# A fused attention and FFN kernel whose opening is issued from a table in another order

## The chip, the cores and the metric

The kernel runs on one NeuronCore of one Trainium2 chip. The core has five engines that run their own instruction streams and meet at semaphores: TensorE (PE in the profile) multiplies matrices into PSUM, which has eight banks; VectorE (DVE) and ScalarE (ACT) do elementwise work; GpSimd (POOL) here issues the loads; SyncE (SP) issues the other DMAs. The metric is the time of one execution on the device in microseconds. Before the change it is 337.19 us, the median of 3 runs (336.64 to 337.4).

## The reference

The function is sliding-window causal attention followed by a SwiGLU block. q, k and v have 8 batches, 8 heads, 576 positions and 64 columns. The heads are joined to 4608 tokens of 512 columns, which feed the second part.

```python
scores = scale * np.matmul(q, k.transpose(0, 1, 3, 2))
mask = (rel >= 0) & (rel < 64)                 # rel: query position less key position
attn = softmax(np.where(mask, scores, -1e9))
x = np.matmul(attn, v).transpose(0, 2, 1, 3).reshape(4608, 512)
g = x @ w_gate                                 # 512 x 1536
val = x @ w_val                                # 512 x 1536
out = (g * sigmoid(g) * val) @ w_out           # 1536 x 512
```

Inputs and output are float32; the kernel computes in bfloat16 with float32 sums.

## The kernel before

The 4608 tokens are 36 chunks of 128 (`n`) and 9 FFN groups of 512 tokens (`c`), four chunks each. For a chunk, `load_qk(n)` and `load_v(n)` put q, k and v into rings of 6, 6 and 10 buffers as bfloat16. `T(n)` transposes q and k on TensorE (line 412) and copies them out of PSUM (line 342 or 344). `TD(n)` does the same with two DMA transposes on SP (lines 425, 428). `S(n)` computes the scores with 24 small matmuls (line 456) and their exponentials on ScalarE (line 466). For chunks 0 to 3, `bias(n)` first writes the mask into the two banks with two matmuls (line 436); otherwise VectorE multiplies the exponentials by the mask (line 471). `A(n)` multiplies with v in two phases (line 505); the row sums come with it, and VectorE takes their reciprocals (line 520) and normalises (line 523) in two halves. `X(n)` transposes the result on TensorE (line 595) and copies it to `xT` (line 604); `XD(n)` does it by a DMA transpose on SP (line 610).

`F(c, f, t0, t1)` is one of the 12 blocks of 128 hidden columns of a group, for the tokens t0 to t1: four matmuls for the gate, four for the value (line 628), a tanh on ScalarE (line 634) and two operations on VectorE (lines 636 and 638) which leave the hidden block in `hT`. `O(c, u)` multiplies 128 tokens of a group with the whole of w_out in 12 matmuls (line 652), evicts the result and stores it. It waits for all 12 hidden blocks and for both halves of w_out (`load_wo`).

Each engine issues its instructions in the order in which `build` calls these functions. Semaphore waits are derived from what each reads and writes. PSUM banks are handed out in rotation, four for the FFN and four for attention, with a list of six at the start. `warm(count)` issues matmuls on a zeroed tile whose result nobody reads.

The opening was written out by hand: 13 warm matmuls, attention of chunks 0 and 1 with five more warm matmuls between, the first two FFN blocks in pieces of 128 tokens, attention of chunks 2 and 3, blocks 2 to 5 of group 0 in halves of 256 tokens, and so on up to group 1. In the loop over `c`, which starts at group 1, `block(n)` stands between the FFN blocks: it loads chunk n + 6, runs `A(n)` with the scores of chunk n + 1 between its two phases, and issues `XD(n)` and `TD(n + 4)`. Group 2 and later take the same path.

All loads of q, k, v and the weights are issued by POOL in program order, and are cast from float32 to bfloat16 as they land. The first two chunks of q and k come by SP and ACT (`first_loads`), and are cast by VectorE and ScalarE.

Of the kernel before, what the change touches and what calls it, by code (L numbers as in the profile page):

```python
# [4 lines left out]
ACTF = mybir.ActivationFunctionType  # L5
# [4 lines left out]
T = B * S  # L10
# [183 lines left out]

class _Kernel:
# [17 lines left out]
    def alloc(self):  # L213
# [39 lines left out]
        self.n_s = 0  # L253
        self.kb = [sb("kb%d" % i, 192, F32) for i in range(3)]
# [7 lines left out]
    def bank(self, kind):  # L262
        kind = "*" if "*" in self.rot else kind
        ids, i = self.rot[kind]
        self.rot[kind] = (ids, i + 1)
        j = ids[i % len(ids)]
        return self.ps[j], ("ps", j)
# [78 lines left out]
    def first_T(self, which):  # L346
# [11 lines left out]
        return tb, bk  # L358

    def first_ev(self, which, n, eng, tb, bk):  # L360
# [39 lines left out]
    def T(self, n, keng="act"):  # L400
        iq, iz = n % self.NQ, n % self.NZ
        kd = self.kT[:, :, 64 + 128 * n:64 + 128 * n + 128]
        kk, qk = [("kT", n, p) for p in range(4)], [("qT", iz, p) for p in range(4)]
        parts = [("kn", self.kn[iq], kd, kk, keng), ("qn", self.qn[iq], self.qT[iz], qk, "act")]
        for group in ([parts] if keng == "act" else [parts[:1], parts[1:]]):
            bank, bk = self.bank("a")
            tb = bank[:, :].bitcast(BF).rearrange("p (w c t) -> p w c t", w=2, c=4)

            def pe(e, group=group, tb=tb):
                for w, part in enumerate(group):  # L410
                    for c in range(4):
                        r = e.transpose(tb[:, w, c, :], part[1][:, 2 * c:2 * c + 2, :], self.ident[:, :])
                return r

            self.g.op("pe", pe, reads=["ident"] + [(g[0], iq, j) for g in group for j in range(2)], writes=[bk])
            for w, (_, _, d, wk, eng) in enumerate(group):
                self.move(eng, d, tb[:, w], [bk], wk)
# [13 lines left out]
    def bias(self, n):  # L431
# [6 lines left out]
        return bb  # L438

    def S(self, n, bb=None, defer=False):  # L440
# [3 lines left out]
        qT, pt = self.qT[iz], self.pt[ip]  # L444
        biased = bb is not None
# [28 lines left out]
        for f in masks:  # L474
            f()

    def A(self, n, nxt=None):
        g = self.g
        ip, ix = n % self.NP, n % 4
# [34 lines left out]
        first = g.op("pe", phase(0), reads=rd, writes=wr)  # L514
        masks = self.S(nxt, None, True) if nxt is not None else []
        g.op("pe", phase(1), reads=rd, writes=wr, after=[first])
        for half, (bank, bk) in enumerate(bb):
# [7 lines left out]
        for f in masks:  # L525
            f()
# [59 lines left out]
    def X(self, n, eng="dve"):  # L586
        g = self.g
        ix, it = n % 4, (n // 4) % self.NX
        xb = self.xb[ix]
# [8 lines left out]
        g.op("pe", pe, reads=["ident", ("xb", ix, 0), ("xb", ix, 1)], writes=[bk])  # L598
        u = n % 4
        xo = self.xT[it][:, :, 128 * u:128 * u + 128]  # L600
        if eng == "dve":
            g.op("dve", lambda e: e.tensor_copy(xo, tb), reads=[bk], writes=[("xT", it, u)])
        else:
            g.op("act", lambda e: e.activation(xo, tb, ACTF.Copy), reads=[bk], writes=[("xT", it, u)])  # L604
# [8 lines left out]
    def F(self, c, f, t0=0, t1=512):  # L613
        g = self.g
        it, ih = c % self.NX, c % self.NH
        xT, hT = self.xT[it], self.hT[ih]
        i = self.n_s % self.NS
        self.n_s += 1
        sig, uu = self.sig[i], self.uu[i]
# [3 lines left out]
        V, vk = self.bank("f")  # L623
# [10 lines left out]
        g.op("act", lambda e: e.activation(sig[:, 0:n], G[:, 0:n], ACTF.Tanh, scale=0.5), reads=[gk], writes=[("sig", i)])  # L634
        g.op("pe", mm(V, self.Wv), reads=xk + [("Wv", f)], writes=[vk])
        g.op("dve", lambda e: e.scalar_tensor_tensor(uu[:, 0:n], sig[:, 0:n], 1.0, G[:, 0:n], ALU.add, ALU.mult),  # L636
# [4 lines left out]
    def O(self, c, u, mid=None, kind="a", eng="act"):  # L641
        g = self.g
        ih = c % self.NH
        hT = self.hT[ih]
        io = (4 * c + u) % self.NO
        ost = self.ost[io]
        OB, ok = self.bank(kind)

        def part(f0, f1):
            def pe(e):  # L650
                for f in range(f0, f1):
                    r = e.matmul(OB[:, :], hT[:, f, 128 * u:128 * u + 128], self.Wo[:, f, :],  # L652
                                 start=(f == 0), stop=(f == NF - 1))
                return r

            g.op("pe", pe, reads=[("hT", ih, f) for f in range(f0, f1)] + [("Wo", f) for f in range(f0, f1)], writes=[ok])

        if mid is None:
            part(0, NF)
        else:  # L660
            part(0, 8)
            mid()
            part(8, NF)
        self.move(eng, ost[:, :], OB[:, :], [ok], [("ost", io)])
        r0 = 512 * c + 128 * u
        g.op("sp", lambda e: e.dma_start(self.out[r0:r0 + 128, :], ost[:, :]), reads=[("ost", io)], dma=True)

# [126 lines left out]
    def general(self):  # L794
# [7 lines left out]
        for n in range(NCH):  # L802
            self.load_qk(n)
            self.load_v(n)
            self.T(n)
            self.S_general(n)
            self.A(n)
            self.X(n, "act")
# [8 lines left out]
    def build(self):  # L817
# [11 lines left out]
        self.load_v(0)  # L829
        self.load_v(1)  # L830
        W(0, 1)
        self.load_qk(2)
        W(1, 2)
        self.load_qk(3)
        self.load_v(2)
        self.load_v(3)
        for f in range(2, 8, 2):
            W(f, f + 2)
        self.load_qk(4)
        W(8, 10)  # L840
        self.load_v(4)
        load(5)
        W(10, 12)
        load(6)
        load(7)

        self.banks("a", [5, 6, 7, 4, 0, 1])
        self.warm(13)
        self.first_cast("k", None, "dve")
        self.first_cast("q", 0, "act")  # L850
        self.first_cast("q", 1, "dve")
        tk = self.first_T("k")
        tq = self.first_T("q")
        b0, b1 = self.bias(0), self.bias(1)
        for n in range(2):
            self.first_ev("k", n, "dve", *tk)
            self.first_ev("q", n, "act", *tq)
# [6 lines left out]
        self.X(0, "act")  # L864
        self.banks("a", [5, 6, 7, 4])
        self.T(2, "dve")
        self.F(0, 0, 0, 128)
        self.X(1, "act")
        self.F(0, 1, 0, 128)
        self.F(0, 0, 128, 256)  # L870
        self.F(0, 1, 128, 256)
        self.T(3, "dve")
        load(8)
        b2 = self.bias(2)
        self.S(2, b2)
        b3 = self.bias(3)
        self.S(3, b3)
        self.F(0, 2, 0, 256)
        self.A(2)
# [168 lines left out]
```

## Time and profile before

| | before |
|---|---|
| median of 3 runs | 337.19 us |
| the profiled execution | 335.81 us |
| its span, first to last instruction | 334.0 us |
| TensorE busy | 320.0 us, 96% |
| VectorE busy | 220.5 us, 66% |
| ScalarE busy | 133.6 us, 40% |
| read from and written to memory | 37.75 MB, 9.44 MB |

The span is what the rows of the profile cover; the time of an execution is some 1.8 us longer. A matmul row gives the start, the time until its result is written, and the number of matmuls that follow each other; the next row starts before the last one's result is out, so work is best read from start to start. In brackets stands how long the engine was idle before and what ended that. Sizes in rows of DMA issues are those in bfloat16.

### The profile page before, as it was taken

Reading aid. Unit: us, or ns where it says so; the run is one execution under the profiler, and the core shown is the slowest. Engines: PE = TensorE matmul, PEld = TensorE weight load, DVE = VectorE, ACT = ScalarE, POOL = GpSimd, SP = SyncE. Lnnn points to the kernel's source line nnn. Section 1 sums busy time; section 2 is a strip of 40 time slices with the busy share of each in tenths; the row PEclk is TensorE's granted clock in tenths of the full one; section 3 lists DMA queues with packets and bytes.
Section 4 is the critical chain, followed back from the end, with each engine's and each line's share of the span. In section 5 each row is a group of like instructions: output and inputs, shape, how many; then the busy total and the mean of one; then the engine's idle time right before and its main releaser. Section 6 shows DMA issues by size and latency. Waiting matters only on the chain.

```text
span 334.0 us, 8383 instructions
## 1 busy us (share of the span) xinstructions
PE 320.0 (96%) x3477; PEld 166.1 (50%) x3515; DVE 220.5 (66%) x481; ACT 133.6 (40%) x248; POOL 110.7 (33%) x141
## 2 busy tenths in 40 slices
PE   8889989998999999999999999999999999999996
PEld 3657557644444444445454545454545444444444
DVE  5558799477666766667777777767676776565510
ACT  2655775353444544444333333333424222332312
POOL 7999993463635453333615151000000000000000
PEclk9999999999999999999999999999999999999999
DMA  9999999999999999999999999915241202000012
GB/s 171 151 190 172 166 196 159 157 168 152 159 169 180 173 153 173 161 151 115 130 125 123 133 123 131 126 51 110 47 105 41 65 31 65 32 31 34 34 66 96
DMA packets 169516, 40.20 MB, mean 120 GB/s; under 512 B 155904, under 2 KB 164992, under 8 KB 169472
## 3 DMA queue, kind: packets, MB, share of 16 engines
q0 software_dynamic: 117312, 18.36, 83.4%
q1 hardware_dynamic: 50976, 20.66, 33.1%
q10 hardware_dynamic: 1184, 0.59, 0.7%
q8 instruction: 29, 0.48, 0.6%
q14 instruction: 15, 0.12, 0.1%
HBM read 37.75 MB, written 9.44 MB: 141 GB/s over the span
## 4 chain that ended last, share of the span: by engine, by line
PE 84%; DMA 4%; POOL 4%; DVE 3%; issue 2%; ACT 1%; SPq 1%; POOLq 0%
PE ps L628 51%; PE ps L652 26%; PE ps L456 3%; DMA qT<-qn 2%; DMA Wv<-in_moe_w_val_dram 2%; PE ps L505 2%; PE ps L552 2%; POOL va L387 1%; DVE uu L636 1%; PE ps L680 1%; DVE xb L523 1%; POOL Wg L393 1%; DVE hT L638 1%; POOL qn L325 1%; POOL kn L325 1%
## 5 line engine op out<-in xcount | busy, mean ns | idle before, releaser
L636 DVE SCALAR_TENSOR_TENSOR uu<-sig,ps 128x512 bf16<-128x512 bf16 (+2 forms) x122 | 76.0, 623 | 62.8 <-ACT sig L634 62.6
L628 PE MATMUL ps<-xT,Wv 128*128 128x512 bf16 (+2 forms) x479 | 112.9, 354 | 1.3 <-DMA Wv<-in_moe_w_val_dram 0.7
L628 PE MATMUL ps<-xT,Wg 128*128 128x512 bf16 (+2 forms) x464 | 108.2, 354 | 5.2 <-issue 3.4
L634 ACT ACTIVATE sig<-ps 128x512 bf16<-128x512 f32 (+2 forms) x122 | 67.2, 551 | 76.6 <-PE ps L628 76.4
L652 PE MATMUL ps<-Wo,hT 128*128 128x512 bf16 x416 | 95.5, 379 | 0.3 <-issue 0.2
L638 DVE SCALAR_TENSOR_TENSOR hT<-uu,ps 128x512 bf16<-128x512 bf16 (+2 forms) x122 | 76.4, 626 | 4.7 <-PE ps L628 0.6
L628 PEld LDWEIGHTS ps<-xT,Wv 128*128 128x128 bf16 x488 | 46.9, 98 | 47.7 <-DMA Wv<-in_moe_w_val_dram 1.0
L628 PEld LDWEIGHTS ps<-xT,Wg 128*128 128x128 bf16 x488 | 44.3, 98 | 43.2 <-ACT xT L604 0.8
L652 PEld LDWEIGHTS ps<-Wo,hT 128*128 128x128 bf16 x420 | 40.9, 98 | 49.0
L325 POOL DMA_DIRECT2D qn<-in_q_dram x38 | 35.2, 944 | 66.5 <-DMA qT<-qn 66.2
L466 ACT ACTIVATE pt<-ps 128x512 bf16<-128x512 f32 x72 | 38.1, 599 | 34.5 <-PE ps L456 33.6
L342 ACT ACTIVATE ost<-ps 128x512 f32<-128x512 f32 (+2 forms) x29 | 16.8, 579 | 73.2 <-PE ps L652 72.2
L387 POOL DMA_DIRECT2D va<-in_v_dram x40 | 37.1, 936 | 24.2 <-PE ps L552 23.1
L325 POOL DMA_DIRECT2D kn<-in_k_dram x38 | 35.3, 936 | 4.3 <-DMA Wo<-in_moe_w_out_dram 3.7
L471 DVE TENSOR_TENSOR pt<-pt,mask 128x512 bf16<-128x512 bf16 x64 | 23.6, 417 | 0.2 <-ACT pt L466 0.2
L344 DVE COPY ost<-ps 128x512 f32<-128x512 f32 (+1 forms) x9 | 5.8, 646 | 23.2 <-PE ps L680 11.8
L523 DVE TENSOR_TENSOR xb<-ps,rc 128x256 bf16<-128x256 f32 x40 | 17.0, 424 | 1.4
L456 PE MATMUL ps<-qT,kT 64*64 64x64 bf16 (+1 forms) x864 | 16.0, 203 | 1.1 <-DMA qT<-qn 1.1
L456 PEld LDWEIGHTS ps<-qT,kT 64*64 64x64 bf16 x864 | 12.5, 108 | 6.6 <-issue 4.0
L505 PE MATMUL ps<-va,pt 64*64 64x65 bf16 x600 | 12.7, 197 | 0.6
L520 DVE RECIPROCAL rc<-ps 128x4 f32<-128x4 f32 x40 | 7.0, 174 | 9.4 <-PE ps L505 9.4
L505 PEld LDWEIGHTS ps<-va,pt 64*64 64x64 bf16 x600 | 8.4, 106 | 8.9 <-issue 4.7
(55 smaller groups left out, 105.3 us busy)
## 6 DMA issues: line engine op xcount, KB each, us to landing
out_dram<-ost SPq DMA_DIRECT2D x35, 256.0 KB, 3.7
va<-in_v_dram POOLq DMA_DIRECT2D x32, 128.0 KB, 10.0
qn<-in_q_dram POOLq DMA_DIRECT2D x30, 128.0 KB, 10.0
kn<-in_k_dram POOLq DMA_DIRECT2D x30, 128.0 KB, 12.5
Wo<-in_moe_w_out_dram POOLq DMA_DIRECT2D x2, 768.0 KB, 15.1
Wg<-in_moe_w_gate_dram POOLq DMA_DIRECT2D x5, 256.0 KB, 8.0
Wv<-in_moe_w_val_dram POOLq DMA_DIRECT2D x5, 256.0 KB, 8.6
fk<-in_k_dram SPq DMA_DIRECT2D x1, 512.0 KB, 5.0
```

What stands on the lines that cost most here:

```text
L325: self.g.op("pool", lambda e, d=d, a=a: e.dma_start(d, a), writes=ks, dma=True)
L387: g.op("pool", lambda e, d=d, a=a: e.dma_start(d, a), writes=ks, dma=True)
L456: r = e.matmul(sv[h][o:o + 64, c, q0:q1], self.kT[ps, c, kk:kk + 64], qT[ps, c, q0:q1], start=not biased, stop=not biased or c == 3 and kk ...
L466: g.op("act", lambda e, po=po, si=si: e.activation(po, si, ACTF.Exp, scale=SCALE), reads=[bk], writes=[pk])
L471: "dve", lambda e: e.tensor_tensor(po, po, m, ALU.mult), reads=[pk, "mask"], writes=[pk]))
L505: r = e.matmul(av[half][ws, j, :], pt[ks, h, ws], vv[ks, h, 0:65], start=key == q[0], stop=key == q[-1])
L523: g.op("dve", lambda e, xo=xo, rb=rb, a=av[half]: e.tensor_tensor(xo, a[:, :, 0:64], rb, ALU.mult), reads=[bk, ("rc", ir)], writes=[("xb", ...
L628: r = e.matmul(bank[:, 0:n], W[:, kk, f * 128:f * 128 + 128], xT[:, kk, t0:t1], start=(kk == 0), stop=(kk == NK - 1))
L634: g.op("act", lambda e: e.activation(sig[:, 0:n], G[:, 0:n], ACTF.Tanh, scale=0.5), reads=[gk], writes=[("sig", i)])
L636: g.op("dve", lambda e: e.scalar_tensor_tensor(uu[:, 0:n], sig[:, 0:n], 1.0, G[:, 0:n], ALU.add, ALU.mult), reads=[("sig", i), gk], writes ...
L638: g.op("dve", lambda e: e.scalar_tensor_tensor(hT[:, f, t0:t1], uu[:, 0:n], 0.5, V[:, 0:n], ALU.mult, ALU.mult), reads=[("uu", i), vk], wr ...
L652: r = e.matmul(OB[:, :], hT[:, f, 128 * u:128 * u + 128], self.Wo[:, f, :], start=(f == 0), stop=(f == NF - 1))
```

## The change

The hand-written opening, and the loop's turn for group 1, are replaced by one table, `OPENING`, of some 300 rows. A row is a method, its arguments and the PSUM banks that it takes, in order. Methods that held several engines' work are split, so that each part has a row: `T` into a transposition of q or of k (`T`) and its copy (`TE`), `A` into its phases (`A0`, `A1`) and the two halves of its normalisation (`R`), `X` into `X` and `XE`, `F` into the matmuls (`FM`), the tanh (`Ft`) and VectorE's part (`Fu`), `O` into `OM` and `OE`, and the masking of the scores into `M`. Each piece computes what it did before.

In the table the loads go v1, qk2, v0, qk3, v2, the first weight block, v3, and then weights and chunks 4 to 7 mixed; blocks 8 and 9 come behind chunk 8's and 10's q and k, the second half of w_out behind chunks 9 and 11. Attention of chunks 0 to 3 comes before the first FFN block. Eleven warm matmuls stand at the start, followed by the bias of chunk 2, and four single ones later. The scores of chunks 8 to 12, the first four output blocks and the attention of chunks 8 to 11 come late in group 1, between its blocks. Some copies go from ScalarE to VectorE and the other way. After the table the loop begins at group 2, with the two rotations of banks set anew.

```diff
+OPENING = [
+    ("warm", (11,), (4,)),
+    ("bias", (2,), (0, 4)),
+    ("first_cast", ("k", None, "dve"), ()),
+    ("first_T", ("k",), (3,)),
...
+    ("bias", (0,), (1, 5)),
+    ("load_v", (1,), ()),
+    ("bias", (1,), (6, 7)),
+    ("load_qk", (2,), ()),
+    ("first_ev", ("k", 0, "act"), ()),
+    ("T", ("q", 2), (3,)),
+    ("load_v", (0,), ()),
...
+    ("S", (0,), ()),
+    ("first_ev", ("q", 1, "dve"), ()),
+    ("S", (1,), ()),
+    ("TE", ("q", 2, "dve"), ()),
+    ("T", ("k", 2), (2,)),
+    ("TE", ("k", 2, "dve"), ()),
+    ("A0", (0,), (3, 5)),
+    ("A1", (0,), ()),
...
+    ("FM", (0, 0, 128, 256, 2), (5, 7)),
+    ("R", (2, 0), ()),
+    ("Ft", (0, 0, 128), ()),
+    ("load_w", ("g", 2, 4), ()),
+    ("warm", (1,), (0,)),
+    ("load_w", ("v", 2, 4), ()),
+    ("FM", (0, 0, 0, 128, 2), (4, 3)),
...
+    ("load_qk", (10,), ()),
+    ("TD", (10,), ()),
+    ("load_w", ("g", 8, 10), ()),
+    ("X", (7,), (4,)),
...
+    ("load_w", ("v", 8, 10), ()),
+    ("load_wo", (0, 6), ()),
+    ("FM", (0, 8, 0, 512, 2), (3, 5)),
...
+    ("OM", (0, 2), (4,)),
+    ("Fu", (1, 7, 0), ()),
+    ("S", (9,), (5, 2)),
...
+    ("S", (12,), (2, 0)),
...
+    ("FM", (1, 11, 0, 512, 2), (1, 4)),
+    ("Ft", (1, 11, 0), ()),
+    ("Fu", (1, 11, 0), ()),
+]
...
     def bank(self, kind):
+        if self.give:
+            return self.given(self.give.pop(0))
...
     def warm(self, count):
-        bank, bk = self.ps[3], ("ps", 3)
+        bank, bk = self.bank("f")
...
-        self.banks("a", [5, 6, 7, 4, 0, 1])
-        self.warm(13)
-        self.first_cast("k", None, "dve")
...
-        self.S(0, b0)
-        self.S(1, b1)
-        self.warm(3)
-        self.A(0)
-        self.warm(2)
-        self.A(1)
...
+        for op, args, give in OPENING:
+            self.give = list(give)
+            getattr(self, op)(*args)
+        self.banks("a", [4, 5, 6, 7])
+        self.banks("f", [0, 1, 2, 3])
...
-        for c in range(1, NFC):
+        for c in range(2, NFC):
```

More of the change, by code (lines that the diff above doesn't have):

```diff
@@ L266, in bank, with given @@
         j = ids[i % len(ids)]
+        return self.ps[j], ("ps", j)
+    def given(self, j):
         return self.ps[j], ("ps", j)
@@ L804, in general @@
             self.load_v(n)
-            self.T(n)
+            for which in "kq":
+                self.T(which, n)
+                self.TE(which, n, "act")
             self.S_general(n)
             self.A(n)
-            self.X(n, "act")
+            self.X(n)
+            self.XE(n, "act")
             if n % 4 == 3:
```

530 lines of the change are left out of this document (361 added, 169 removed), and 18 rows, old and new, of the table OPENING.

## The prediction

> **What bounds the kernel now.** I read the page first, then the busy time by stage, then TensorE's waits before the second FFN group, then single rows for prices.
>
> ```profile
> span 334.0 us, 8383 instructions
> ...
> PE 320.0 (96%) x3477; PEld 166.1 (50%) x3515; DVE 220.5 (66%) x481; ACT 133.6 (40%) x248; POOL 110.7 (33%) x141
> ...
> PE   8889989998999999999999999999999999999996
> ...
> DMA  9999999999999999999999999915241202000012
> ```
>
> TensorE (PE) is the bound: 96% of the span. Its row of tenths falls short of 9 almost only in the first ten slices. The DMA row shows that the transfers never rest there either, so work that starts earlier must find its data already landed.
>
> ```profile
> 0.00:6.72 6.72, 5.52 (x13) 1.91 (x14) 3.16 (x19) 1.54 (x3) 4.74 (x13) 1.00 0.91 177
> 6.72:18.50 11.78, 10.80 (x237) 7.16 (x236) 6.78 (x21) 7.93 (x17) 11.78 (x16) 1.00 1.92 155
> 18.50:30.36 11.86, 10.58 (x152) 8.77 (x153) 9.24 (x26) 5.71 (x15) 11.86 (x17) 1.00 1.67 185
> 30.36:48.40 18.04, 17.08 (x287) 10.13 (x287) 14.00 (x33) 13.52 (x27) 18.04 (x23) 1.00 1.93 177
> 48.40:66.00 17.60, 16.38 (x224) 11.69 (x226) 12.36 (x34) 7.25 (x17) 8.06 (x12) 1.00 1.94 161
> 66.00:85.55 19.55, 17.82 (x237) 9.04 (x239) 13.51 (x35) 9.89 (x18) 9.90 (x12) 1.00 1.77 161
> 85.55:334.00 248.45, 241.86 (x2333) 117.34 (x2360) 161.50 (x318) 87.75 (x155) 46.35 (x56) 1.00 0.97 104
> ```
>
> The columns are stretch, its length, busy PE, weight loads, VectorE (DVE), ScalarE (ACT), GpSimd (POOL), granted clock, DMA share, GB/s. The third FFN group (c = 2) starts at 85.55 us, and from there both programs issue the same instructions. Everything is decided before: from 6.72 to 85.55 us PE is busy 10.80+10.58+17.08+16.38+17.82 = 72.66 of 78.83 us, so 6.17 us are idle.
>
> ```profile
> PE ps L456 <- DMA qT<-qn: 1.1, 1, 1.1
> PE ps L628 <- issue: 1.0, 6, 0.2
> PE ps L628 <- DMA Wv<-in_moe_w_val_dram: 0.7, 1, 0.7
> PE ps L628 <- DVE uu L636: 0.6, 1, 0.6
> ...
> PE ps L628 <- DMA Wg<-in_moe_w_gate_dram: 0.4, 1, 0.4
> PE ps L595 <- DVE xb L523: 0.2, 1, 0.2
> ```
>
> These waits (total, times, longest) are the prize: 1.1 us for chunk 12's qT at 78 us, 1.1 us for the weights of blocks 2 and 3 at 19 us, 0.6 us and, for X(6), 0.2 us at 49 us. The 1.0 us of "issue" follows each attention and is not touched.
>
> **The change part by part.** The prices on PE:
>
> ```profile
> 1.20 5.73 PE L373 MATMUL ps<-wz 128*128 128x512 bf16 x13 [1.20 <-DVE wz L287]
> ...
> 20.77 1.29 PE L505 MATMUL ps<-va,pt 64*64 64x65 bf16 x64
> ...
> 30.36 0.39 PE L412 MATMUL ps<-ident,kn 128*128 128x128 bf16 x4
> 30.59 0.39 PE L412 MATMUL ps<-ident,qn 128*128 128x128 bf16 x4
> ...
> 54.15 0.60 PE L628 MATMUL ps<-xT,Wg 128*128 128x256 bf16 x4
> ...
> 55.02 0.60 PE L628 MATMUL ps<-xT,Wg 128*128 128x256 bf16 x4
> ...
> 56.86 0.44 PE L456 MATMUL ps<-qT,kT 64*64 64x128 bf16 x24
> ...
> 83.82 1.03 PE L628 MATMUL ps<-xT,Wg 128*128 128x512 bf16 x4
> ...
> 85.55 1.02 PE L628 MATMUL ps<-xT,Wg 128*128 128x512 bf16 x4
> ```
>
> Start to start, a whole FFN block (gate and value) is 85.55-83.82 = 1.73 us, half a block 55.02-54.15 = 0.87, four transposes 30.59-30.36 = 0.23; the scores of a chunk (S) are some 0.4, the products of one chunk (A) half of 1.29, some 0.61. Splitting a block costs nothing (two halves make 1.74).
>
> The start: 11 warm matmuls and the two of chunk 2's bias take the place of 13 warm ones at 0.44 us, so PE reaches the first transposes at 6.72 us as before. The five warm matmuls of the middle become four of one each, at some 0.22 us (a quarter of the 0.86 us of a gate's four); they stand where PE would wait, so I take nothing for them; the bound is ±0.9 us.
>
> The loads: POOL issues them in order, and the new order is v1, qk2, v0, qk3, v2, W0, v3, W2-3, W1, qk4, W4-5, g6-7, qk5, v5, v4, v6-7, qk7, qk6, W10-11, v6, v7, qk8, qk10, W8-9, first half of Wo, qk9, v8, qk11, second half of Wo.
>
> ```profile
> 3.37 1.90 POOL L387 DMA_DIRECT2D va<-in_v_dram  x2 [0.30 <-issue]
> ...
> 34.47 1.19 POOL L387 DMA_DIRECT2D va<-in_v_dram  x1
> 35.33 1.97 POOL L398 DMA_DIRECT2D Wo<-in_moe_w_out_dram  x2
> ...
> 38.69 1.24 POOL L387 DMA_DIRECT2D va<-in_v_dram  x1
> ...
> 46.48 1.31 POOL L387 DMA_DIRECT2D va<-in_v_dram  x1
> ```
>
> and, in windows of the DMA view around 5 to 13, 14, 34, 37 (two rows) and 44 us (KB, median us to landing):
>
> ```profile
> va<-in_v_dram POOLq DMA_DIRECT2D x2, 128.0 KB, 4.9
> ...
> Wv<-in_moe_w_val_dram POOLq DMA_DIRECT2D x1, 256.0 KB, 5.9
> ...
> va<-in_v_dram POOLq DMA_DIRECT2D x1, 128.0 KB, 9.9
> ...
> Wo<-in_moe_w_out_dram POOLq DMA_DIRECT2D x1, 768.0 KB, 17.1
> ...
> va<-in_v_dram POOLq DMA_DIRECT2D x1, 128.0 KB, 17.4
> ...
> va<-in_v_dram POOLq DMA_DIRECT2D x2, 128.0 KB, 22.8
> ```
>
> Up to 19 us: POOL is at about 0.9 us for each load of 128 KB, so v0, the fourth, is issued near 6.1 and lands 4.9 later, near 11.0. Chunk 0's products wait for it (some 0.7 us of idle that was filled by warm matmuls). From then VectorE drives:
>
> ```profile
> 12.41 0.18 DVE L520 RECIPROCAL rc<-ps 128x4 f32<-128x4 f32 x1
> ...
> 12.97 0.17 DVE L520 RECIPROCAL rc<-ps 128x4 f32<-128x4 f32 x1
> ```
>
> Eight normalisations at 0.56 us (12.97-12.41) and three copies of some 0.4 run from 11.75; with waits for exponentials and for v3 (landing near 16) chunk 3 is normalised near 18.5. The value weights of blocks 2 and 3, issued near 12.7, land near 18.6. So block (0,2) starts near 18.8, beside 18.9 (gate) and 20.24 (value) before. By then the new order has half of block 0 and four finished chunks; the old one had halves of two blocks, and still owed A of chunks 2 and 3 and two transposes (1.2+0.4 us) and the weight waits (1.1). That is 1.6+1.1-0.9 = 1.8 us ahead.
>
> Up to the ninth block: from here loads gate. I count bytes. In the old order the load at 34.47 landed 9.9 later, at 44.4; with it 6016 KB had landed, all weights of gate and value among them. The value weights of blocks 8 and 9 are at 6144 KB in the new order with the same mix, so they land near 45.3 by rate. Four DMA transposes (chunks 8 and 10) now run from 41 us, ahead of most of it; I add 0.7, 46.0. The chain on PE: the keys of chunk 6 land near 34.9 (45.3 less four weight loads of 1.3 and six of 0.87 us, the paces of this stream), then blocks 6, 10, 11, three halves, S of 6 and 7, A of 6 and 7, three transposes, blocks 8 and 9: 5x1.73+3x0.87+0.8+0.8+0.7 = 13.6 us, so block 9 ends near 48.7; by the weights, 46.0+0.86+1.73 = 48.6. I take 48.7. At 48.40 us the old order had not done X(6), A(7), X(7) and half of block (1,5): 0.23+0.61+0.23+0.87 = 1.9 us.
>
> Up to 85.55: the old stretch of 37.15 us less these 1.9, less the waits of 0.2 (X(6)), 0.6 and 1.1 us, is 33.3 us. S(12) comes last of the late scores, behind two output blocks and two more FFN blocks than S(9); its transpose goes out behind that of chunk 8's output, near 63, and PE reaches it near 75, so the 1.1 us go. Four output blocks, S of 8 to 12 and X of 10 and 11 are the same work in another order. For waits of the new order between its split attentions I add 0.8 us (from none to 2). The group ends at 48.7+33.3+0.8 = 82.8 against 85.55: 2.7 us less. Chunk 13's transpose then has about 1 us to spare behind XD(9) on SP.
>
> SP's and DVE's part: SP issues the same transposes; VectorE takes some ten copies of 0.4 us from ScalarE, beside 14.00 busy of 18.04 us in the fullest long stage. They lie beside PE work; if that cover is gone they cost up to 4 us, which I hold in the upper end.
>
> The sum: the profiled execution has a span of 334.0 and a time of 335.81 us, the median of the runs is 337.19. 335.81-2.7 is 333.1; from the median, 334.5 us.
>
> **The transposes beside the weights: row and rule.** The old order has such a stretch: from 43.5 us the pair for chunk 8 is in flight,
>
> ```profile
> 43.50 1.30 SPq L425 DMA_TRANSPOSE kT<-kn  x1
> ```
>
> and the 1.5 MB of Wo behind the load that lands at 44.4 are in at 36.2+17.1 = 53.3 us: 8.9 us, where weights alone (1.3 us for 256 KB, the gap between the landings near 18.8 and 20.15 of gate and value of blocks 2 and 3) would take 7.8. Hence my 0.7 us. [...]
>
> **The rivals.**
> The output weights become the gate (slower). The second half of Wo, one wait for all output blocks, moves 768 KB down the stream. In the old order it lands at 53.3 us with 7552 KB; the twelve loads after it, up to 46.48+22.8 = 69.3, take 1.33 us each beside transposes, and the last nine of them, from 38.69+17.4 = 56.1, take 1.47, where 0.87 is the pace without. In the new order Wo ends at 8320 KB, near 61 us by the old stream, near 62.5 with two more transposes ahead; PE reaches the first output block 14.7 us after block 9, at 63.4. If from 41 us on all loads go at the pace of 1.47 (1.7 times as long), W8-9 lands near 48.5, half of Wo near 55.4, five loads later 62.8, and Wo is whole at 69.7, where PE has come to 65.8: 3.9 us of waiting after 2.4 us lost at block 8, 334.5+6.3 = 340.8. At 1.33 the same steps give 1.4 and 1.6 us, 337.5. It decides for slower once Wo lands after 66. For it: landing times that rise to 22.8 us. Against: the 8.9 us above.
>
> The gaps drop the clock (slower). PE would do the 6 us of work between 11 and 18.8 us at half pace; some 3 us of gaps take up half: 3 us lost, 337.5, and more if the low pace holds past it. The trace shows full pace after every gap of up to 1.1 us (warm matmuls go at 0.44 us each at the start, a gate's four at 0.22 later), and my longest gap is 0.9 us. [...]
>
> The opening is hidden by the loads (no change). If each load of the new order lands 1.5 us later than I count and VectorE's ten copies delay the transposes of chunks 4 to 7, all but the lost wait at 78 us is given back: 336.5 to 337.3.
>
> All gates are met early: no wait beyond 18.8 us, 0.8 less and up to 1 us less again: 332.8.
>
> **How the numbers follow.** The forecast with its better case has 0.72 (332.8 to 336.4 by itself), the loads hiding it 0.10, Wo as the gate 0.10, equal shares 0.04, the clock 0.04. 334.5 us is the likeliest. Runs of this kernel tell 0.2% (0.7 us) from no change. Faster takes the forecast and the better part of the hidden case, 0.76; the same 0.08, the rest of it and the mild end of Wo; slower Wo, equal shares and the clock, 0.16. The range of 332.7 to 338.2 leaves out the worst of Wo and little below.
>
> **What would show it.** Right: PE reaches block (0,2) at 18 to 19.5 us, ends block 9 at 48 to 50 and starts the third group (c = 2) at 82 to 84; no wait for qT at S(12); PE's wait list shows va and Wv by less than 1.5 us together. Wrong: 128-wide or 512-wide matmuls at double spacing between 9 and 20 us; PE waiting for Wo at the first output block, for Wv at block 8, or for DVE's xb by more than 2 us in all.

## The result, and the profile after

The changed kernel takes 335.0 us, the median of 9 runs (334.32 to 335.62). The kernel before took 336.32 us in 9 runs beside it (335.4 to 337.4). The medians differ by 1.3 us; the ratio is 0.9957, with a 95% interval of 0.9936 to 0.9977, that is 0.43% faster. The forecast was 334.5 us and 2.7 us faster. The time itself came closer than the gain, and that is luck, because two errors oppose each other: the gain was half of what I said, and the median of the kernel before is 0.9 us lower in nine runs than it was in the three that I started from.

One thing is to be mended in what stands above: the text says that four single warm matmuls stand in the table. There are three, two near 19 us and one near 28 us.

The profiled execution of the changed kernel took 335.52 us, the second longest of its nine. The page of its profile, the lines that answer those of before, and one line of the list of DMA queues (queue and kind: packets, MB, share of 16 engines):

```profile
span 333.5 us, 8363 instructions
...
PE 319.0 (96%) x3470; PEld 166.9 (50%) x3511; DVE 225.7 (68%) x494; ACT 126.8 (38%) x235; POOL 111.1 (33%) x141
...
PE   7789899998999999999999999999999999999997
...
DMA  9999999999999999999999999915151212100012
...
q8 instruction: 28, 0.46, 0.5%
```

TensorE is still the bound and still falls short in the first ten slices only. VectorE has 5 us more and ScalarE 7 us less than before, both with room to spare. The busy time by stage, cut where the prediction cut it (stretch, length, busy PE, weight loads, DVE, ACT, POOL, granted clock, DMA share, GB/s):

```profile
0.00:6.84 6.84, 5.11 (x13) 1.74 (x14) 3.00 (x18) 1.49 (x2) 4.86 (x13) 1.00 0.90 176
6.84:20.44 13.60, 10.16 (x288) 7.31 (x289) 8.53 (x27) 7.22 (x15) 13.60 (x19) 1.00 1.86 151
20.44:51.98 31.54, 29.41 (x432) 21.07 (x435) 27.18 (x73) 17.26 (x37) 29.49 (x36) 1.00 1.87 169
51.98:67.06 15.08, 14.92 (x150) 9.87 (x152) 12.32 (x30) 5.79 (x14) 2.90 (x4) 1.00 1.84 155
67.06:85.74 18.68, 17.51 (x262) 9.46 (x264) 13.11 (x33) 7.23 (x14) 12.51 (x15) 1.00 1.83 156
85.74:333.50 247.76, 241.85 (x2333) 117.49 (x2360) 161.55 (x318) 87.82 (x155) 47.70 (x57) 1.00 0.95 106
```

The stage from 6.84 to 20.44 us holds all the attention of four chunks, and in it TensorE is idle for 13.60-10.16 = 3.44 us. Block (0,2) starts at 20.44 us, block (0,9) ends at 51.98, and the third group starts at 85.74; forecast were 18.8, 48.7 and 82.8. What TensorE waits for between 6.7 and 86 us:

```profile
PE ps L781 <- issue: 2.3, 2, 1.2
PE ps L833 <- ACT pt L791: 0.8, 1, 0.8
PE ps L781 <- DVE ost L667: 0.8, 1, 0.8
PE ps L677 <- DVE ck L667: 0.5, 1, 0.5
PE ps L833 <- DVE kT L667: 0.5, 1, 0.5
PE ps L677 <- ACT cq L665: 0.3, 1, 0.3
...
```

(Lines have moved: L781 is the matmul of the scores, L833 that of the products with v, L978 that of the FFN blocks.) The waits that the change was to remove are gone: no wait of TensorE in this list ends with a DMA any more, neither the 1.1 us for chunk 12's qT nor the 1.1 us for the weights of blocks 2 and 3. In their place stands one line that the sum did not have: 2.3 us in two waits at the scores, put down to "issue", that is, to nothing that the profile shows. The rows around them, from the timeline of TensorE:

```profile
13.98 0.32 PE L833 MATMUL ps<-va,pt 64*64 64x65 bf16 x16
14.31 0.40 PE L948 MATMUL ps<-ident,xb 128*128 128x128 bf16 x4
14.64 0.41 PE L781 MATMUL ps<-qT,kT 64*64 64x128 bf16 x21
16.30 0.22 PE L781 MATMUL ps<-qT,kT 64*64 64x64 bf16 x2 [1.25 <-issue]
...
17.81 0.71 PE L833 MATMUL ps<-va,pt 64*64 64x65 bf16 x32 [0.81 <-ACT pt L791]
...
38.77 0.81 PE L781 MATMUL ps<-qT,kT 64*64 64x128 bf16 x41
40.64 0.26 PE L781 MATMUL ps<-qT,kT 64*64 64x64 bf16 x7 [1.06 <-issue]
```

TensorE stops in the middle of the scores of chunk 3, after 21 of 24 matmuls of one function whose inputs are all there, and again in the scores of chunks 6 and 7, after 41 of 48, that is after the 17th of chunk 7. The program waits for the inputs of a chunk's scores ahead of the first of them, not among its like. That is what the experiments are about.

In this pair of profiled executions the third group starts 0.19 us later than before (85.74 and 85.55), so the pair does not show the gain of the medians. The last row of matmuls starts later too, at 328.16 us, before at 328.03; the span is 0.5 us shorter by what follows it alone.

### The profile page after: what moved, and what is told of

It reads as the page before. It is cut to its first block, busy times and chain, and to the rows that moved or that the text cites. A ratio compares the mean times of both kernels' runs of the same rounds, so it can differ in the third digit from the quotient of the medians.

```text
span 333.5 us, 8363 instructions
## 1 busy us (share of the span) xinstructions
PE 319.0 (96%) x3470; PEld 166.9 (50%) x3511; DVE 225.7 (68%) x494; ACT 126.8 (38%) x235; POOL 111.1 (33%) x141
## 4 chain that ended last, share of the span: by engine, by line
PE 91%; issue 2%; DVE 2%; DMA 2%; ACT 1%; ACTq 0%
PE ps L978 54%; PE ps L1018 26%; PE ps L781 4%; PE ps L833 2%; DMA fq<-in_q_dram 2%; PE ps L906 2%; PE ps L731 1%; PE ps L1050 1%; DVE uu L1006 1%; PE ps L948 1%; DVE hT L1008 1%; ACT pt L791 1%; PE ps L760 0%; ACT sig L997 0%; DVE ost L667 0%
## 5 line engine op out<-in xcount | busy, mean ns | idle before, releaser
L978 PE MATMUL ps<-xT,Wv 128*128 128x512 bf16 (+2 forms) x479 | 112.8, 354 | 0.5
L978 PE MATMUL ps<-xT,Wg 128*128 128x512 bf16 (+2 forms) x463 | 108.0, 353 | 3.6 <-issue 2.4
L978 PEld LDWEIGHTS ps<-xT,Wv 128*128 128x128 bf16 x488 | 47.2, 98 | 46.3 <-DVE hT L1008 0.4
L978 PEld LDWEIGHTS ps<-xT,Wg 128*128 128x128 bf16 x488 | 44.8, 98 | 41.9 <-ACT qT L665 0.2
L711 POOL DMA_DIRECT2D va<-in_v_dram x40 | 35.9, 928 | 23.9 <-PE ps L906 19.8
L665 ACT ACTIVATE ost<-ps 128x512 f32<-128x512 f32 (+2 forms) x27 | 15.6, 577 | 67.6 <-PE ps L1018 66.6
L667 DVE COPY ost<-ps 128x512 f32<-128x512 f32 (+1 forms) x11 | 7.2, 654 | 23.2 <-PE ps L1050 11.8
L781 PE MATMUL ps<-qT,kT 64*64 64x64 bf16 (+1 forms) x864 | 16.5, 203 | 3.4 <-issue 2.3
L781 PEld LDWEIGHTS ps<-qT,kT 64*64 64x64 bf16 x864 | 12.7, 108 | 9.0 <-issue 5.9
L833 PE MATMUL ps<-va,pt 64*64 64x65 bf16 x600 | 12.0, 196 | 1.7 <-ACT pt L791 0.8
L833 PEld LDWEIGHTS ps<-va,pt 64*64 64x64 bf16 x600 | 8.2, 106 | 8.8 <-issue 4.0
```

The lines of the kernel that those rows point to most:

```text
L711: g.op("pool", lambda e, d=d, a=a: e.dma_start(d, a), writes=ks, dma=True)
L781: r = e.matmul(sv[h][o:o + 64, c, q0:q1], self.kT[ps, c, kk:kk + 64], qT[ps, c, q0:q1], start=not biased, stop=not biased or c == 3 and kk ...
L833: r = e.matmul(av[half][ws, j, :], pt[ks, h, ws], vv[ks, h, 0:65], start=key == q[0], stop=key == q[-1])
L978: r = e.matmul(bank[:, 0:n], W[:, kk, f * 128:f * 128 + 128], xT[:, kk, t0:t1], start=(kk == 0), stop=(kk == NK - 1))
```

## The experiments

**Two theories.** The refill theory: TensorE waits for its own instructions. They come by a DMA queue of their own, the line q8 above: 0.46 MB in 28 packets is 16 KB a packet. The records hold 3470+3511 = 6981 matmuls and weight loads of TensorE; 6981/28 is 249 for each packet. Counted in the order of the program, each weight load, each matmul and each separate wait as one, the two stops lie at instruction 450 and 1217, which is 767 apart: three times 256, to within one. In the trace the packets of q8 start at 13.80, 20.74, 28.14 and 38.15 us, and the two stops end 2.50 and 2.49 us after the first and the fourth of them. Between 13.98 and the stop, 41 matmuls with their weight loads, 82 instructions, are issued in about 0.9 us (rows above). In FFN blocks, at 0.216 us for a matmul of 512 columns, 82 instructions last some 9 us, which is longer than those 2.5 us and would hide such a transfer. So, by this theory, a stop stands where the count reaches 450 plus a multiple of 256 just behind a run of small attention matmuls (what the engine had loaded ahead of the first counted instruction is not known), and a kernel with some more instructions ahead of that place has it elsewhere.

The clock theory, the rival: the gaps between 11 and 20 us let the granted clock of TensorE fall in some executions (three of the nine above have a mean of 0.995), and that is what eats the gain.

**The changed kernel again** (no edit), for a second trace.

> The changed kernel, nothing edited: a second profile. Both theories: 334.3 to 335.6 us. Refill theory (the two gaps of TensorE marked issue, 1.25 us in S(3) near 15 us and 1.06 us in S(7) near 39.6 us, are waits for the next 16 KB of its own instructions, which come by DMA): both gaps stand again after the 21st matmul of S(3) and the 17th of S(7), within 0.3 us of these lengths, since the instruction numbers are the same. Chance theory (a transfer of data or a semaphore that happened to be late in that one execution): they are somewhere else or gone.

Measured: 334.76 us, the median of 12 runs (333.77 to 336.41); ratio 0.9955 (0.9933 to 0.9977). The profiled execution, 336.08 us, had a mean granted clock of 0.99. Its busy time in steps of 3.41 us, half of the 6.82 us that it spends at half clock, and rows of its timeline:

```profile
13.79:17.20 3.41, 2.11 (x66) 1.22 (x64) 1.31 (x6) 1.18 (x3) 3.41 (x6) 1.00 1.54 153
17.20:20.61 3.41, 2.47 (x46) 2.24 (x48) 2.52 (x9) 0.78 (x3) 3.41 (x5) 0.50 1.70 163
20.61:24.02 3.41, 3.41 (x22) 2.55 (x21) 1.89 (x6) 1.26 (x3) 3.41 (x6) 0.50 1.73 183
24.02:27.43 3.41, 3.41 (x41) 3.14 (x39) 2.61 (x8) 1.55 (x5) 3.41 (x6) 1.00 1.92 174
```

```profile
14.80 0.41 PE L781 MATMUL ps<-qT,kT 64*64 64x128 bf16 x21
16.34 0.22 PE L781 MATMUL ps<-qT,kT 64*64 64x64 bf16 x2 [1.12 <-issue]
...
18.72 0.61 PE L978 MATMUL ps<-xT,Wg 128*128 128x128 bf16 x4
19.12 0.63 PE L978 MATMUL ps<-xT,Wv 128*128 128x128 bf16 x4
...
22.11 1.06 PE L978 MATMUL ps<-xT,Wg 128*128 128x256 bf16 x4
22.96 1.06 PE L978 MATMUL ps<-xT,Wv 128*128 128x256 bf16 x4
...
41.38 0.88 PE L781 MATMUL ps<-qT,kT 64*64 64x128 bf16 x48
```

Both theories find something here. The stop at 21 of 24 score matmuls is at the same place in a second execution. The second stop is not there, though by the refill theory I expected both: all 48 score matmuls of chunks 6 and 7 run through. The packets fit this. The fourth starts at 39.37 us, 2.01 us ahead of these scores, where it was 0.62 us (38.15 to 38.77) in the first profile; 2.5 us on from 39.37 is 41.87, about when that 17th score is due. Equal instruction numbers are thus not enough for a stop: between these two executions the time from the packet's start to the scores differs, and with it the work that lies ahead of the boundary. And from 17.20 to 24.02 us the granted clock is one half: half a block takes 22.96-22.11 = 0.85 us for each of its two parts, where it took 0.44 at full clock, and a gate of 128 columns 0.40 instead of 0.22. Eight of the 12 executions had a mean clock of 0.995 or less; their median is 335.25 us, that of the four at full clock 334.54.

**Moving the instruction count.** The 11 warm matmuls of 512 columns become 44 of 128, which is the same work in 33 matmuls more, 66 instructions with their weight loads:

```diff
+        n, cols, lw = (44, 128, 128) if count > 1 else (count, 512, 128)
-            for _ in range(count):
-                r = e.matmul(bank[:, :], self.wz[:, 0:128], self.wz[:, :], start=True, stop=True)
+            for _ in range(n):
+                r = e.matmul(bank[0:lw, 0:cols], self.wz[:, 0:lw], self.wz[:, 0:cols], start=True, stop=True)
```

> The 11 warm matmuls of 512 columns are issued as 44 of 128 columns: the same time at the slow pace, 66 instructions more ahead of everything else on TensorE. Refill theory: the points where a new 16 KB of instructions is needed move 66 instructions earlier in the work, to before A0(2) near 14 us and into the start of S(6); the gap in S(3) is gone, up to 0.8 us may appear near 14 us, at most 0.4 us near 38 us; 333.0 to 334.5 us, 0.5 to 2 below the changed kernel. Data theory (the gaps belong to S(3) and S(7): their q, k or banks): the gaps stay in S(3) and S(7) and the time stays at 334.6 to 335.4 us.

Measured: 334.35 us, 9 runs (333.76 to 334.99); ratio 0.9937 (0.9917 to 0.9957). Both stops are gone from the scores of chunks 3 and 7, and a new one stands near 45 us. Its timeline:

```profile
38.01 0.88 PE L782 MATMUL ps<-qT,kT 64*64 64x128 bf16 x48
...
41.10 0.88 PE L834 MATMUL ps<-va,pt 64*64 64x65 bf16 x64
41.91 0.61 PE L979 MATMUL ps<-xT,Wg 128*128 128x256 bf16 x4
42.35 0.60 PE L979 MATMUL ps<-xT,Wv 128*128 128x256 bf16 x4
42.79 0.49 PE L979 MATMUL ps<-xT,Wg 128*128 128x256 bf16 x3
44.84 0.28 PE L979 MATMUL ps<-xT,Wg 128*128 128x256 bf16 x1 [1.55 <-issue]
...
84.68 1.03 PE L979 MATMUL ps<-xT,Wg 128*128 128x512 bf16 x4
```

All 48 score matmuls of chunks 6 and 7 run through. The new stop, in an FFN block of all places, has 64 small products (128 instructions) shortly ahead of it. It lies at instruction 1408 by the old count, which is 450+4x256-66: where the refill theory puts it. I had looked only at the places that the shift would free, and had not expected it; the clock theory gives no stop there. The third group starts at 84.68 us, 1.06 earlier.

**A second shift**, 88 warm matmuls of 64 by 64, 154 instructions more, which brings other boundaries into the attention:

> The 11 warm matmuls of 512 columns are issued as 88 of 64 by 64: the same time, 154 instructions more ahead. Refill theory: the points move to A(1) near 12.3 us (a gap of up to 1.7 us there), to FFN blocks near 17 and 27 us (none), and to the end of A(5) near 35 us (up to 0.7 us); none in S(3) and S(7); 333.3 to 335.0 us. Data theory: gaps in S(3) and S(7) as before, 334.6 to 335.4 us.

```diff
+        n, cols, lw = (88, 64, 64) if count > 1 else (count, 512, 128)
```

Measured: 334.18 us, 9 runs (332.29 to 336.5); ratio 0.9936 (0.9903 to 0.9969). Timeline:

```profile
12.18 0.22 PE L834 MATMUL ps<-va,pt 64*64 64x65 bf16 x3
13.21 0.69 PE L834 MATMUL ps<-va,pt 64*64 64x65 bf16 x29 [0.80 <-issue]
...
17.24 0.68 PE L834 MATMUL ps<-va,pt 64*64 64x65 bf16 x27 [0.81 <-ACT pt L792]
18.48 0.28 PE L834 MATMUL ps<-va,pt 64*64 64x65 bf16 x5 [0.57 <-issue]
```

The stops are now in the products of chunk 1 and of chunk 3, at instructions 296 and 552 of the old count: 450-154 and 450+256-154. The places follow the count; which of them cost time was only half foreseen, as I had put the second boundary into FFN blocks without a stop, and a stop near 35 us that I allowed for is not there. Seven of its nine executions had a mean clock of 0.995 or less; the two at full clock have a median of 332.46 us.

**The kernel before, shifted** by 78 instructions (its 13 warm matmuls as 52 of 128 columns), to see whether splitting the warm matmuls does anything by itself:

```diff
+        n, cols = (4 * count, 128) if count > 5 else (count, 512)
-            for _ in range(count):
-                r = e.matmul(bank[:, :], self.wz[:, 0:128], self.wz[:, :], start=True, stop=True)
+            for _ in range(n):
+                r = e.matmul(bank[:, 0:cols], self.wz[:, 0:128], self.wz[:, 0:cols], start=True, stop=True)
```

> The kernel before, its 13 warm matmuls issued as 52 of 128 columns: the same time, 78 instructions more ahead. Refill theory: the old order has its attention in shorter bursts, each refill has some 2.5 us of slower work ahead of it wherever it falls; no gap over 0.7 us marked issue appears, and the time is 335.6 to 337 us, as the kernel before. If a gap over 1 us appears, the luck of the place is worth as much as the change. Data theory: 336.3 us, within 0.4, unchanged.

Measured: 335.79 us, 12 runs (335.08 to 337.98), ratio 0.9981 (0.996 to 1.0002). No stop over 0.2 us appears, and no difference from the kernel before can be told over all runs. Among the executions at full clock the median is 335.32 us against 336.0, so it is not excluded that smaller warm matmuls are worth up to 0.7 us by themselves. The profiles show no such gain at the start: in those of the changed order the first transposes begin at 6.71 to 6.84 us with whole warm matmuls and with small ones alike.

**Filling the gaps.** Two warm matmuls ahead of the products of chunk 0, and three ahead of those of chunk 3, keep TensorE busy where it waited. The periods at half clock seen so far last 6.82 us (the changed kernel again) and 3.41 us (the shift of 154, from 18.27 us).

```diff
+    ("warm", (2,), (3,)),
     ("A0", (0,), (3, 5)),
...
+    ("warm", (3,), (6,)),
     ("A0", (3,), (6, 1)),
```

> The changed kernel with five warm matmuls more, where TensorE waits anyway: two ahead of A0(0) (near 10.5 us), three ahead of A0(3) (near 17 us). Clock theory (windows of 3.4 us with too little work on TensorE between 10 and 20 us make the granted clock fall to half for one or two windows, in about half of the executions of the changed kernel, which show a mean clock of 0.995 or 0.99): the share of executions under 1.0 falls from 11 of 21 to 2 in 10 or less, and the median falls by 0.3 to 0.8, to 334.0 to 334.6 us; the refill gap in S(3) or the phase after it stays. If the clock falls whatever fills the gaps: the share stays near one half and the median at 334.8 to 335.2 us.

Measured: 334.94 us, 12 runs (333.78 to 338.39); ratio 0.9966 (0.9942 to 0.999). One of the 12 executions had a mean clock of 0.995 or less, where it was 16 of 33 over the three sets without the edit, so the gaps seem to feed the drop of the clock, as the clock theory has it. But the median is not lower, and not in the expected 334.0 to 334.6. The two warm matmuls ahead of the stop are four instructions, and it moves by just that, from behind the 21st to behind the 19th score matmul of chunk 3. The second stop is not in this profile: the fourth packet starts at 36.52 us, 2.48 us ahead of the scores at 39.00. The first one grows:

```profile
14.54 0.41 PE L783 MATMUL ps<-qT,kT 64*64 64x128 bf16 x19
16.51 0.24 PE L783 MATMUL ps<-qT,kT 64*64 64x128 bf16 x3 [1.56 <-issue]
```

**The shift that fits**, 50 instructions (36 warm matmuls of 156 columns), chosen from the count so that slow blocks lie ahead of most boundaries up to the third group; and the same with the fillers:

```diff
+        n, cols, lw = (36, 156, 128) if count > 5 else (count, 512, 128)
```

> The 11 warm matmuls of 512 columns as 36 of 156: the same time, 50 instructions more ahead. Refill theory: the points where new instructions are needed fall 50 earlier than in the changed kernel, at the front of S(3) (up to 0.8 us), in a block after S(4), in the front part of S(6) or ahead of it and in the block after A(7), where slow blocks lie ahead of most; gaps marked issue over 0.5 us sum to under 1 us up to 86 us, where the changed kernel had 2.3; 333.0 to 334.2 us. Otherwise 334.6 to 335.2 us as the changed kernel.

> Both: 50 instructions more ahead and the five warm matmuls in the gaps. If refill and clock are two separate losses, the gains add: 332.2 to 333.8 us, at least 8 of 10 executions at a mean clock of 1.0. If the gaps of the refills are what makes the clock fall, this is no better than the shift alone, 333.0 to 334.2 us.

Measured: 333.96 us with the shift, 7 runs (333.54 to 335.05), ratio 0.9932 (0.9907 to 0.9956), and no wait marked "issue" above 0.22 us. With the fillers on top 334.61 us, 12 runs (333.64 to 336.65), ratio 0.9966 (0.9943 to 0.999): their ten instructions push the boundary back among small matmuls, and stops of 1.74 us (at 15.78) and 0.57 us (at 45.09) come back. That is outside both expectations, and 0.65 us above the shift alone, with the same small warm matmuls and 10 of the 12 executions at full clock; the two differ by the stops and the five fillers. The two edits cannot be added without counting again.

**Without the three single warm matmuls** (three rows of the table removed, which moves the count by six):

```diff
-    ("warm", (1,), (0,)),
...
-    ("warm", (1,), (0,)),
...
-    ("warm", (1,), (0,)),
```

> The changed kernel without its three single warm matmuls (two near 19 us, one near 28 us). Clock theory: less work in the windows around 17 to 20 us, so the mean clock is under 1.0 in more executions than the 11 of 21, and the median rises by 0.2 to 1 us, to 335.1 to 336 us. Rival, that these three cost time on TensorE and do nothing for the clock: 0.2 to 0.6 us faster, 334.3 to 334.7 us.

Measured: 334.45 us, 9 runs (333.48 to 335.84); ratio 0.9942 (0.992 to 0.9964). Four of nine executions were at 0.995 or less, no more than with them. There is no sign that they hold the clock; the clock theory's expectation was wrong here. The count shows again. The single ones stand behind the scores of chunk 3 and ahead of those of chunk 7; the first stop leaves two score matmuls behind it as in the changed kernel, the second leaves four instead of seven, three matmuls or six instructions later:

```profile
15.90 0.22 PE L778 MATMUL ps<-qT,kT 64*64 64x64 bf16 x2 [0.97 <-issue]
...
41.49 0.25 PE L778 MATMUL ps<-qT,kT 64*64 64x64 bf16 x4 [1.26 <-issue]
```

**The three side by side on one chip**: the changed kernel, the shift of 50 again, and the shift without the single warm matmuls (39 of 144 columns at the start, so that the count is the same behind them).

```diff
-    ("warm", (1,), (0,)),
...
-    ("warm", (1,), (0,)),
...
-    ("warm", (1,), (0,)),
...
-        n, cols, lw = (36, 156, 128) if count > 5 else (count, 512, 128)
+        n, cols, lw = (39, 144, 128) if count > 5 else (count, 512, 128)
```

> The changed kernel as it is, for a direct comparison on one chip with the next two. Refill theory: the two waits of TensorE for its own instructions stand at S(3) and S(7) as before, each 0.9 to 1.7 us, and the time is 334.6 to 335.2. Chance theory (the better times of the shifted kernels are the spread between calls): the three kernels of this call have medians within 0.4 us of each other.

> The changed kernel with 36 warm matmuls of 156 columns for 11 of 512 at the start, 50 more instructions for the same work. Refill theory: no wait marked issue over 0.3 us ahead of the third group, and 0.6 to 1.2 us less than the unshifted kernel of this call: 333.7 to 334.2. Chance theory: within 0.4 us of the unshifted kernel.

> As the kernel before it, without the three single warm matmuls, and with 39 of 144 columns at the start, so that from the second refill on the instructions have the same numbers. If the single warm matmuls buy nothing: the same time as the kernel before it within 0.3 us, and no more of its executions under full clock. If they hold the clock: more of its executions under full clock, and 0.3 to 0.8 us slower.

| | median (runs) | range | ratio to before (95%) | clock 0.995 or less |
|---|---|---|---|---|
| the changed kernel | 334.92 (12) | 333.93 to 336.85 | 0.9967 (0.9945 to 0.9988) | 5 |
| shift of 50 | 333.54 (6) | 332.86 to 334.86 | 0.9930 (0.9905 to 0.9954) | 1 |
| and no single warm matmuls | 333.02 (6) | 332.61 to 334.5 | 0.9916 (0.9891 to 0.9940) | 0 |

The unshifted kernel has its two stops again, 1.29 and 1.33 us, at 16.40 and 41.01 us. The shifted one, from its timeline:

```profile
14.86 0.41 PE L782 MATMUL ps<-qT,kT 64*64 64x128 bf16 x22
...
19.20 0.60 PE L979 MATMUL ps<-xT,Wg 128*128 128x256 bf16 x4
...
21.81 0.38 PE L979 MATMUL ps<-xT,Wv 128*128 128x256 bf16 x2 [0.26 <-issue]
...
37.95 0.88 PE L782 MATMUL ps<-qT,kT 64*64 64x128 bf16 x48
...
50.37 0.60 PE L979 MATMUL ps<-xT,Wg 128*128 128x256 bf16 x4
...
83.29 1.03 PE L979 MATMUL ps<-xT,Wg 128*128 128x512 bf16 x4
```

The largest stop left up to there is 0.26 us, and the third group starts at 83.29 us, 2.45 earlier than in the changed kernel's first profile, 2.26 earlier than in its third, and 0.5 behind my 82.8. Of the 2.26 us 1.6 are left at the end (spans of 331.8 and 333.4 us); the rest is lost in small steps behind it. The chance theory, that the better times of the shifted kernels are the spread between sets of runs, is out: 334.92 and 333.54 differ by 1.4 us, a little more than the 0.6 to 1.2 expected. Part of that may be the clock, since five of 12 executions were below full clock and one of six; among the executions at full clock the medians are 334.49 and 333.42. The kernel without the single warm matmuls beats both kernels of this case: 3.3 us under the kernel before by the medians, 0.84% by the ratio. That it beats the one with them by 0.5 us is not settled by six runs of each.

## Why the prediction was right or wrong, point by point

**The direction and the range held.** The median lies within 332.7 to 338.2, and 0.43% is beyond the 0.2% that I took as no change. Of the signs named beforehand, the three times of the profile missed: block (0,2) at 20.44 us for 18 to 19.5, the end of block 9 at 51.98 for 48 to 50, the third group at 85.74 for 82 to 84. The wait for qT at the scores of chunk 12 is gone, and va and Wv cost less than 1.5 us.

**The waits named as the prize were the prize.** Those for qT, for the weights and for the FFN hidden block at X(6) are gone. The transfers did not take their place: no wait of TensorE up to the third group ends with a DMA in the profiled execution. In the third profile of the changed kernel 0.7 us do, for v0 ahead of the products of chunk 0, as the prediction had it; in the shifted kernels it is up to 1.2 us (va and qT without the single warm matmuls). So three rivals are not seen: the output weights as the gate, equal shares between transposes and weights, and an opening hidden by the loads. For the equal shares, which the chances give 0.04, no run shows loads at half pace beside transposes: in the profiled execution the value weights of blocks 8 and 9 are issued at 35.73 us and land 11.4 us later, near 47.1, where I had 46.0, with transposes in flight from 42.78 us on. Block 9 ends at 51.98 us, but no wait for Wv stands ahead of it, so its delay has another cause: in the shifted kernel it ends at 50.37.

**Up to the third block: 18.8 forecast, 20.44 measured.** Of the 1.64 us, 1.25 are the stop in the scores of chunk 3. Without it, in the kernels shifted by 66 and by 50, the block starts at 19.02 and 19.20 us. What is left is the small waits that I had not listed (0.3 us for cq at the first transposes, part of the 0.8 us for the exponentials ahead of A(3)).

**Up to the ninth block: 48.7 forecast, 51.98 measured.** Half of the miss is handed down. Of the rest, 1.06 us are the second stop. But the shifted kernel, with no stop but 0.26 us, still needs 50.37-19.20 = 31.17 us for this stretch, where I had 29.9: I took the place of block 9 from the landing of chunk 6's keys and the weights, and neither was the gate: no wait there ends with a DMA. Of the 31.17 us TensorE is busy for 30.26; the other 0.91 are small waits that the sum does not have, 0.26 of them the stop and 0.26 one for VectorE ahead of the scores of chunk 4. The products of chunks 6 and 7 stand in the sum at 0.8 us, where its own price of 0.61 a chunk gives 1.2; they took 0.81 (42.88 to 43.69), so the slip did no harm.

**From there to the third group: 33.3+0.8 forecast, 33.76 measured.** Near the forecast, but by luck. The wait of that size in the first profile, 0.8 us for "DVE ost", the bank of an output eviction which moved to VectorE, ahead of the scores of chunk 12, is in none of the other profiles of this order. In the third one of the changed kernel the stretch takes 85.55-52.34 = 33.21 us, in the shift of 50 83.29-50.37 = 32.92 us with TensorE busy throughout. So the 0.8 us was not needed there, and this offsets most of the 1.3 us missing from the stretch before.

**The step that failed** is a term missing from the sum. For waits of the new order I added 0.8 us, behind block 9; up to block 9 nothing stands for waits of TensorE for its own instructions. The new order cost two such stops there, 2.3 us in the first profile and 2.6 in the third, in place of none above 0.2 us before. The runs show it by moving: counts shifted by 66, 154, 4 and -6 instructions ahead of a stop, and each time the stop went with the count, in steps of 256. With the stops out of the way (the shift of 50) the order is worth 2.8 us by the medians of one set (333.54 against 336.32) and 2.3 by those of the other (333.96 against 336.22), 0.7% by either ratio: near the 2.7 us that I forecast for it. The shift took 1.4 us off the median, 1.1 at full clock, which is less than the 2.3 to 2.6 us of the stops; where the rest goes is not shown, nor how much of the 1.4 us the smaller warm matmuls bring by themselves.

The 1.0 us of "issue" that the prediction calls untouched is another thing, and I read it wrongly. These waits, of 0.16 us each, stand ahead of rows of three matmuls where four belong, or of 11 for 12: one record of a matmul is missing in each, and its time shows as idle. The third profile of the changed kernel has as many matmuls as weight loads, 3511 of each, where the first has 3470 matmuls, and behind 88 us the first lists 15 such waits and the third none.

```profile
PE 323.5 (97%) x3511; PEld 166.9 (50%) x3511; DVE 225.7 (68%) x494; ACT 126.8 (38%) x235; POOL 110.8 (33%) x141
```

**The clock rival** had 0.04 from me, on the ground that full pace held after gaps of up to 1.1 us and that my longest gap was 0.9. It is not what halved the gain: among the executions at full clock alone, the changed kernel gains 1.5 us (334.54 against 336.0) and 1.7 us (334.49 against 336.18) in the two sets with the experiments. But it happens: in 16 of the 33 executions of the changed kernel, over its three sets of runs, the mean granted clock was 0.995 or less, and in 18 of 73 of the kernel before, beside the experiments. Its price is smaller than my 3 us: medians 0.7 us apart (335.25 and 334.54) in one set of runs and 1.4 (335.91 and 334.49) in another; in the first set the three executions below full clock are not slower (334.69 against 335.01). My error was to judge it from one execution. The profiled executions of both kernels were at full clock.

**The warm matmuls** were rightly taken at nothing: without the three of the middle (I counted four) the time is no longer.

**What stays open.** The profiled executions of the changed kernel at full clock, 335.52 and 335.43 us, are above the medians of its runs at full clock (335.01, 334.54 and 334.49 in the three sets). Which part is shorter in those is not shown, as there is no trace of one. No profile of the changed kernel shows TensorE ahead of the kernel before: the last row of matmuls starts at 328.16, 328.74 and 328.09 us in its three profiles and at 328.03 before, so the gain of the medians is not located. The two executions of the shift of 154 at full clock, 332.46 us, are below those of the shift of 50 (333.42), though a profile of the former shows two stops; that is not explained. Why a transfer of instructions starts as late as it does was not tried. Nor is the condition for the drop of the clock settled.

## What to carry to other kernels

A wait marked "issue" in the middle of equal matmuls, with their data long there, can be a wait for instructions: compare its place with the count of instructions, and with the packets of the instruction queue, before putting it down to the order. One of 0.16 us, ahead of a row that is one matmul short, was here a record missing from the profile. The stops of 0.57 to 1.74 us in these runs stand in runs of small attention matmuls, or behind 64 of them with 11 to 14 FFN matmuls between. Where they fall was a matter of how many instructions stand ahead, and that could be changed: warm matmuls cut into other pieces gave 1.1 to 1.4 us. An edit that only adds a few instructions can lose by that alone: ten of them brought back stops of 1.74 and 0.57 us. So when costing an edit, count what it does to the numbers of the instructions behind it.

## What the runs showed of the hardware that was not expected

Instructions of TensorE come in packets of 16 KB (0.46 MB in 28), with 256 of them to a packet by the steps in which the stops move. Up to 90 us all stops of over 0.25 us, in every profile, end 2.24 to 2.54 us after the start of a packet (14.27 to 16.51 us with the fillers, 19.46 to 21.81 in the shift of 50, 13.80 to 16.30 in the changed kernel). Not every packet brings one: in the changed kernel's first profile nine start before 90 us, and two of them have a stop. Ahead of the stops of 0.26 and 0.38 us in the last two kernels stand FFN matmuls; behind runs of 64-row matmuls the stops reach 1.74 us.

The granted clock went to one half without any long pause. In the 3.41 us ahead of the drop at 17.20 us TensorE was busy for 2.11 us, 62%, and its longest gap there was 1.12 us. With the fillers a like stretch, cut in the same steps from the time at which full clock was granted (6.96 us there, 5.09 here), has less work and a longer gap in it, 1.18 us, and did not bring a drop:

```profile
15.33:18.74 3.41, 1.92 (x60) 1.20 (x62) 1.69 (x6) 1.08 (x2) 3.41 (x6) 1.00 1.37 159
18.74:22.16 3.42, 3.34 (x43) 2.83 (x41) 3.01 (x11) 1.54 (x4) 3.42 (x5) 1.00 2.02 170
```

So neither the busy share of such a stretch nor the longest gap decides it alone. The half clock lasted 6.82 us in the second profile of the changed kernel and 3.41 us, half of that, in the profiles of the shifts of 154 and 50. What sets it off is not shown.
